# A decode attention kernel that streams its cache: a branch at the head of TensorE's program, and five sets of small loads

## The chip, the cores and the metric

The kernel runs on one core of a Trainium2 chip. The metric is the device time of one execution in microseconds (us); lower is better. A profile is one execution taken by the hardware profiler. It names the engines PE (TensorE; PEld is its weight load), DVE (VectorE), ACT (ScalarE), POOL (GpSimd) and SP (SyncE, which here only issues transfers and waits). Transfers run on the core's 16 DMA engines, whoever issues them.

## The reference, cut to what matters

One decode step for two sequences: attention with 32 query heads over 8 cached key and value heads of 32768 positions each, gated by a small network. Everything is float32, and each element of the caches is read once.

```python
xn = _layernorm(x)                                   # x: 2 x 1 x 512
q  = (xn @ wq) as 2 x 32 heads x 128
k, v = caches, each of 2 x 8 heads x 32768 x 128     # 4 query heads share one
p  = softmax(q k^T / sqrt(128));  o = p v
s  = o @ wo
h  = relu(xn @ w1 + b1) ** 2
return x + s * silu(h @ w2 + b2)
```

## The kernel before

All weights and both caches are packed on the host into matrices of 128 rows, and SP loads them in the order of their use through two slots in SBUF of 128 x 16384 floats (8.4 MB each). The stream has 66 loads: `wq`, then `wm` (the two matrices of the small network), and then, for each of the 16 pairs of sequence and cached head, two halves of the keys (`kt`) and two halves of the values (`vt`). Behind the last load SP issues seven pieces of `wo` (4 MB down to 128 KB), which lie in a buffer of their own.

A load may be issued when the matmuls that read its slot two loads earlier are done. `load` (L163 to L170) makes SP wait for the token of those matmuls and then issue; `release` (L177 to L188) is called where such a block of matmuls ends and issues the next load. SP's program is thus a row of waits and issues. Its counter `issued[0]` holds the number of loads so far, the one being issued included.

PE, ACT and DVE do not run through unrolled code. The class `Looped` records their operations (so that every recorded operation has line L63), and after all is recorded, three parts are emitted for each of them: what stands ahead of the loop (`ahead`), a hardware loop of 16 rounds whose body is one pair (`round`), and what follows (`rest`).

- Ahead of the loop: layer norm; the queries from the first load (`sc<-slot,xT`), transposed (`tp`); the small network from the second load (`wb<-slot,xT`, `wb<-slot,hT`, `wb<-o_sb,selq`).
- A round: the scores of both key halves into two PSUM banks (`sc<-slot,qz`); the row maximum, spread by a transpose (`ms<-ident,r`); the exponential on ACT; transposes of the probabilities (`tp<-ident,prob`); the sums (`ms<-selh,l`); the values times the probabilities (`o_ps<-slot,pT`); a transpose and a sum of the partial results (`ot<-ident,o_sb`).
- After the loop: `wo` times the heads (`wb<-wo_sb,oT` and `sc<-wo_sb,oT`), as its pieces arrive; then the gate, the residual and the store.

A matmul in float32 of this program stands in the trace as two matmuls, each with a weight load. The loop is opened with `head_slot={PE: 0}`, which makes its first instruction the first of a block of 256 instructions: an alignment mark and a branch stand ahead of it (the `ISA` and `UNCONDITIONAL_BRANCH` of L449).

Of the kernel before, what the change touches and what calls it, by code (L numbers as in the profile page):

```python
# [124 lines left out]
def build(nc, x22, x8, kt, vt, wq, wm, wo, out):  # L125
    pe, act, dve = (Looped(nc, e, n) for e, n in ((nc.tensor, "pe"), (nc.scalar, "act"), (nc.vector, "dve")))
    pool, sp = (Engine(nc, e, n) for e, n in ((nc.gpsimd, "pool"), (nc.sync, "sp")))
# [7 lines left out]
    def sb(name, *shape):  # L135
        return nc.alloc_sbuf_tensor(name, [P, *shape], F32)
# [18 lines left out]

    slot_sem = [nc.alloc_semaphore(f"slot{i}") for i in range(NSLOT)]
    piece_sem = [nc.alloc_semaphore(f"piece{i}") for i in range(len(PIECES) + 2)]
    small_sem, xe_sem, out_sem = (nc.alloc_semaphore(n) for n in ("small", "xe", "out"))
    count = [0] * NSLOT
    free = [None] * NSLOT  # L160
    issued = [0]

    def load(src, width):  # L163
        i = issued[0] % NSLOT
        issued[0] += 1
        if free[i] is not None:
            sp.wait(free[i])
        count[i] += 16
        nc.sync.dma_start(slots[i][:, 0:width], src).then_inc(slot_sem[i], 16)  # L169
        return i, (slot_sem[i], count[i])  # L170

    stream = [load(wq, SLOT)]
    nc.sync.sem_clear(out_sem)
    stream.append(load(wm, 2 * FJ * D))
    todo = [(x[s, u], SLOT) for s in range(NS) for x in (kt, vt) for u in range(2)]

    def release(token):  # L177
        free[stream.pop(0)[0]] = token
        if todo:
            stream.append(load(*todo.pop(0)))  # L180
            if not todo:
                h = 0
                for n, sem in zip(PIECES, piece_sem):
                    nc.sync.dma_start(wo_sb[:, h * D:(h + n) * D], wo[h * P:(h + n) * P].rearrange("(p h) e -> p (h e)", h=n)).then_inc(sem, 16)
                    h += n
                for u in range(2):
                    nc.sync.dma_start(wo_sb[:, h * D + u * NG * HN:h * D + (u + 1) * NG * HN],
                                      wo[h * P + u * HN:h * P + (u + 1) * HN].rearrange("r (t e) -> (r t) e", t=2)).then_inc(piece_sem[len(PIECES) + u], 16)  # L188
# [3 lines left out]
    t = pool.done(g.memset(ident[:, :], 0.0))  # L192
# [11 lines left out]
    for u in range(2):  # L204
# [5 lines left out]
    t = dve.done("tensor_reduce", selh[:, :], ident[:, :].rearrange("p (a h) -> p h a", h=REP), axis=AX.X, op=ALU.add)  # L210
# [10 lines left out]
    t = pe.done()  # L221
    dve.wait(t)
    t = dve.done("tensor_copy", xs[:, :], ms[:, 0:22])
    pe.wait(t, t_one)
    mm(ms[:, 32:40], mean[:, :], xs[:, 0:8], start=True, stop=True)
    t = pe.done()
    dve.wait(t)
    t = dve.done("tensor_reduce", st[:, 2:4], ms[:, 32:40].rearrange("p (d b) -> p b d", b=B), axis=AX.X, op=ALU.add)
    dve.wait(t)
    t = dve.done("tensor_tensor", xc[:, :].rearrange("p (d b) -> p d b", b=B), xs[:, 0:8].rearrange("p (d b) -> p d b", b=B),  # L230
                                 st[:, None, 2:4].to_broadcast([P, ND, B]), op=ALU.add)
    dve.wait(t)
    t = dve.done("tensor_mul", sq[:, :], xc[:, :], xc[:, :])
    pe.wait(t)
    mm(ms[:, 64:72], mean[:, :], sq[:, :], start=True, stop=True)
    t = pe.done()
    dve.wait(t)
    t = dve.done("tensor_reduce", st[:, 4:6], ms[:, 64:72].rearrange("p (d b) -> p b d", b=B), axis=AX.X, op=ALU.add)
    dve.wait(t)
    t = dve.done("tensor_scalar", st[:, 6:8], st[:, 4:6], -1.0, 1e-5, op0=ALU.mult, op1=ALU.add)  # L240
    act.wait(t)
    t = act.done("activation", st[:, 8:10], st[:, 6:8], AF.Sqrt)
    dve.wait(t)
    t = dve.done("reciprocal", st[:, 10:12], st[:, 8:10])
# [5 lines left out]
    i, t = stream[0]  # L250
# [6 lines left out]
    t = pe.done()  # L257
# [3 lines left out]
    for f in range(2):  # L261
# [3 lines left out]
        t = pe.done()  # L265
# [14 lines left out]
    def scores(u):  # L280
        i, t = stream[0]
        pe.wait(t, t_set, t_exp[u])
        for j in range(NJ):
            for c in range(NG):
                lo = (c * NJ + j) * W
                mm(sc[u][32 * c:32 * c + 32, :], qz[:, 28 - 4 * j:60 - 4 * j], slots[i][:, lo:lo + W],
                         start=(j == 0), stop=(j == NJ - 1))
        t = pe.done()
        release(t)
        dve.wait(t)  # L290
        return t, dve.done("tensor_reduce", rm[:, u:u + 1], sc[u][:, :], axis=AX.X, op=ALU.max)
# [44 lines left out]
    for s in range(NS):  # L336
# [4 lines left out]
        t_s, t = scores(1)  # L341
# [3 lines left out]
        t = dve.done("tensor_reduce", r1[:, :], rm[:, :], axis=AX.X, op=ALU.max)  # L345
        pe.wait(t, *([t_rs] if t_rs else []))
        tr(ms[:, :P], r1[:, :].to_broadcast([P, P]), ident[:, :])
        t = pe.done()
        dve.wait(t)
        t = dve.done("tensor_reduce", mh[:, :], ms[:, :P].rearrange("p (a h) -> p h a", h=REP), axis=AX.X, op=ALU.max)  # L350
        dve.wait(t)
        t = dve.done("tensor_mul", mm4[:, :], mh[:, :], seln[:, :])
        dve.wait(t)
        t = dve.done("tensor_reduce", nm[:, :], mm4[:, :], axis=AX.X, op=ALU.add)
# [5 lines left out]
        for u in range(2):  # L360
# [3 lines left out]
            t = pe.done()  # L364
# [4 lines left out]
        t = pe.done()  # L369
        dve.wait(t)  # L370
        t_rs = dve.done("reciprocal", rs[:, :], ms[:, :REP])
        for u in range(2):
            i, t = stream[0]
            pe.wait(t, t_pT[u], t_osb)
            for n in range(32):
                y = n % NG
                k, r = divmod(n, 8)
# [36 lines left out]
    for n, sem in zip(PIECES, piece_sem):  # L414
        pe.wait((sem, 16))
        for h in range(h, h + n):
            if h < WIDE:
                c = h % NG
                mm(wb[32 * c:32 * c + 32, :], heads(h, 0), wt[:, h, :], start=(h < NG), stop=(h >= WIDE - NG))
                if h == WIDE - 1:  # L420
                    t = pe.done()
# [15 lines left out]
    t = pe.done()  # L437
    dve.wait(t, t_gate)
    t = dve.done("tensor_mul", yb[:, :], gate[:, :], acc[:, :HN])
    dve.wait(t, (xe_sem, 32))  # L440
    t = dve.done("tensor_add", yb[:, :], yb[:, :], xb[:, :HN])
    sp.wait(t)
    nc.sync.dma_start(out, yb[:, :]).then_inc(out_sem, 16)
    used = sorted(x.num for x in [e.sem for e in (pe, act, dve, pool, sp)] + slot_sem + piece_sem + [small_sem, xe_sem])
    nc.sync.sem_clear(range(used[0], used[-1] + 1))
    nc.sync.wait_ge(out_sem, 16)
    for e in (pe, act, dve):
        e.ahead()
    with nc.Fori(0, NS, 1, engines=OrderedEngineSet([e.e.engine for e in (pe, act, dve)]), head_slot={pe.e.engine: 0}) as i:  # L449
# [46 lines left out]
```

## Time and profile before

| What | us |
|---|---|
| median of 3 runs | 1303.39 |
| lowest and highest | 1303.38, 1303.41 |
| span of the profiled execution | 1301.8 |
| PE matmul busy | 672.3 |
| PE weight loads busy | 208.2 |
| ACT busy | 78.9 |
| DVE busy | 49.5 |

The span runs from the first to the last instruction of the program in the profile. The runs are timed without a profiler and hold a little more at both ends, so the table has both. Over the span the core reads 561.01 MB, a mean of 431 GB/s. Shares of the DMA engines are means over all 16; a share of 0.25 can be four engines at work or sixteen at a quarter. A packet is put down to the stretch in which it starts or runs by its own times, so that in very short stretches a share can pass 1.

### The profile page before, as it was taken

The page shows a single profiled execution, that of the slowest core. Times are in us where ns is not written, and L with a number is a line of the kernel's source. Part 1 is how long each engine was busy: PE and PEld are TensorE (multiplying, and loading weights), DVE is VectorE, ACT ScalarE, POOL GpSimd, SP SyncE. Part 2 cuts the span into 40 slices and gives each one's busy share as a digit, 9 for nine tenths or more (in the row PEclk, how much of TensorE's full clock was granted, in tenths as well). Part 3 has the DMA queues.
Part 4 walks back from the last instruction along what each step waited for, and adds up shares of the span by engine and source line. Part 5 has one row for each costly group of instructions (what it writes and reads, how often), then busy time and mean ns, then how long its engine had stood idle before and what let it go on. Part 6 is the DMA issues. An engine that isn't in the chain of part 4 may idle for free.

```text
span 1301.8 us, 10286 instructions
## 1 busy us (share of the span) xinstructions
PE 672.3 (52%) x4671; PEld 208.2 (16%) x4671; DVE 49.5 (4%) x166; ACT 78.9 (6%) x138; POOL 5.4 (0%) x29
## 2 busy tenths in 40 slices
PE   3456455535546545545635544554554654554565
PEld 1111111201112111111212111111111211111122
DVE  0000000000000000000000000000000000000000
ACT  1010010100001010010101001010010101001010
POOL 0000000000000000000000000000000000000000
PEclk9776667677677778677767767767767767767778
DMA  9999999999999999999999999999999999999998
GB/s 406 433 446 423 445 423 447 419 441 429 429 441 427 443 425 445 423 447 419 439 431 427 443 427 443 425 445 421 447 421 439 431 427 443 427 443 425 445 421 362
DMA packets 10726, 561.13 MB, mean 431 GB/s; under 512 B 1339, under 2 KB 1633, under 8 KB 1889
## 3 DMA queue, kind: packets, MB, share of 16 engines
q1 hardware_dynamic: 10656, 561.03, 99.7%
q8 instruction: 5, 0.08, 0.0%
q10 hardware_dynamic: 65, 0.02, 0.0%
HBM read 561.01 MB, written 0.03 MB: 431 GB/s over the span
## 4 chain that ended last, share of the span: by engine, by line
DMA 75%; PE 24%; issue 1%; DVE 0%; ACT 0%; SPq 0%; DVEq 0%; ACTq 0%
DMA slot<-in_vt 36%; DMA slot<-in_kt 36%; PE sc L63 12%; PE o_ps L63 11%; DMA slot<-in_wm 3%; PE wb L63 1%; DVE hT L63 0%; PE ot L63 0%; DVE o_sb L63 0%; ACT o_sb L63 0%; DVE yb L63 0%; SPq L169 0%; DVE t L63 0%; DVE oT L63 0%; DVEq L101 0%
## 5 line engine op out<-in xcount | busy, mean ns | idle before, releaser
L63 PE MATMUL sc<-slot,qz 128*32 128x512 f32 x2048 | 295.3, 741 | 300.0 <-DMA slot<-in_kt 300.0
L63 PE MATMUL o_ps<-slot,pT 128*16 128x512 f32 x2048 | 294.3, 739 | 208.9 <-DMA slot<-in_vt 208.9
L63 PEld LDWEIGHTS sc<-slot,qz 128*32 128x32 f32 x2048 | 81.1, 133 | 503.4 <-issue 503.4
L63 PEld LDWEIGHTS o_ps<-slot,pT 128*16 128x16 f32 x2048 | 69.3, 113 | 420.6 <-issue 420.6
L63 ACT ACT_TABLE_LOAD x19 | 24.4, 1283 | 650.5 <-DVE nm L63 647.6
L63 PE MATMUL tp<-ident,prob 128*128 128x128 f32 x136 | 31.0, 397 | 53.3 <-ACT prob L63 53.2
L63 DVE TENSOR_REDUCE rm<-sc 128x1 f32<-128x512 f32 x32 | 22.1, 692 | 575.1 <-PE sc L63 575.1
L63 ACT COPY o_sb<-o_ps 128x512 f32<-128x512 f32 x16 | 9.4, 585 | 504.7 <-PE o_ps L63 504.7
L63 PEld LDWEIGHTS tp<-ident,prob 128*128 128x128 f32 x136 | 23.8, 204 | 57.9 <-issue 56.1
L63 DVE TENSOR_REDUCE t<-ot 128x4 f32<-128x64 f32 x16 | 3.6, 224 | 524.0 <-PE ot L63 524.0
L63 ACT ACTIVATE prob<-sc,nm 128x512 f32<-128x512 f32 x32 | 21.7, 682 | 0.2
L63 ACT COPY pT<-tp 128x512 f32<-128x512 f32 x32 | 18.7, 585 | 13.8 <-PE tp L63 13.8
L63 PE MATMUL sc<-slot,xT 128*32 128x512 f32 x64 | 8.4, 684 | 17.5 <-DMA slot<-in_wq 17.5
L63 PE MATMUL ot<-ident,o_sb 128*128 128x128 f32 x64 | 10.1, 280 | 13.7 <-ACT o_sb L63 13.7
L63 PEld LDWEIGHTS ms<-selh,l 128*128 128x128 f32 x64 | 15.6, 334 | 0.0
L63 PE MATMUL ms<-ident,r 128*128 128x128 f32 x16 | 4.7, 294 | 20.0 <-DVE r L63 20.0
L63 PE MATMUL ms<-selh,l 128*128 128x4 f32 x64 | 13.7, 319 | 0.0
L63 PEld LDWEIGHTS ot<-ident,o_sb 128*128 128x128 f32 x64 | 6.7, 141 | 27.9 <-issue 27.9
L63 PE MATMUL wb<-slot,xT 128*32 128x448 f32 x32 | 4.6, 738 | 6.6 <-DMA slot<-in_wm 6.6
L273 POOL COPY qz<-qT 128x4 f32<-128x4 f32 x16 | 3.0, 186 | 1167.3 <-PE sc L63 1137.3
L63 PEld LDWEIGHTS ms<-ident,r 128*128 128x128 f32 x16 | 2.1, 133 | 34.1 <-issue 34.1
L63 PE MATMUL wb<-wo_sb,oT 128*32 128x512 f32 x54 | 6.2, 596 | 0.7 <-DVE oT L63 0.7
(62 smaller groups left out, 55.6 us busy)
## 6 DMA issues: line engine op xcount, KB each, us to landing
slot<-in_wm SPq DMA_DIRECT2D x1, 7168.0 KB, 38.3
wo_sb<-in_wo SPq DMA_DIRECT2D x1, 4096.0 KB, 39.3
wo_sb<-in_wo SPq DMA_DIRECT2D x1, 2048.0 KB, 43.7
wo_sb<-in_wo SPq DMA_DIRECT2D x1, 1024.0 KB, 45.8
slot<-in_kt SPq DMA_DIRECT2D x32, 29.2
slot<-in_vt SPq DMA_DIRECT2D x32, 29.2
wo_sb<-in_wo SPq DMA_DIRECT2D x1, 512.0 KB, 46.6
wo_sb<-in_wo SPq DMA_DIRECT2D x1, 256.0 KB, 46.7
```

The source lines that it names most:

```text
L63: instruction = getattr(self.e, name)(*[x(i) if callable(x) else x for x in args], **kw)
L273: return pool.done(g.tensor_copy(qz[:, 28:32], qT[:, b, hkv, :]))
```

## The change

Three things are added.

- PE's program gets an alignment mark for a block of 256 instructions at its head, and PE, ACT and DVE a branch to a new part, `second_block`, in which all that was there before follows. The padding that the alignment needs is jumped over.
- Behind the loads with the numbers 3, 4, 6, 8 and 42 SP issues fifteen small loads, for k = 1 to 15: k rows of 16 + k floats (68 to 124 bytes a row) from `wo` into a buffer `mark` that nothing reads.
- SP's last wait, ahead of the store of the result, waits for these 75 loads too.

```diff
+    mark, mark_sem = sb("mark", 75, 32), nc.alloc_semaphore("mark")
...
         nc.sync.dma_start(slots[i][:, 0:width], src).then_inc(slot_sem[i], 16)
+        if issued[0] in (at := (3, 4, 6, 8, 42)):
+            for k in range(1, 16):
+                nc.sync.dma_start(mark[0:k, 15 * at.index(issued[0]) + k - 1, 0:16 + k], wo[0:k, 0:16 + k]).then_inc(mark_sem, 16)
         return i, (slot_sem[i], count[i])
...
-    sp.wait(t)
+    sp.wait(t, (mark_sem, 5 * 15 * 16))
     nc.sync.dma_start(out, yb[:, :]).then_inc(out_sem, 16)
...
     nc.sync.wait_ge(out_sem, 16)
+    nc.tensor.addr_align(256, offset=0, max_nops=0)
+    nc.br("second_block", engines=OrderedEngineSet([e.e.engine for e in (pe, act, dve)]))
+    nc.switch_bb("second_block")
     for e in (pe, act, dve):
         e.ahead()
```

The instructions in their order show where the additions stand. First PE, from the start of its program to the scores of the loop's first key half; before:

```order
L63 MATMUL ms<-ident,small 128x22
L63 MATMUL ms<-xs,mean 128x8
L63 MATMUL ms<-sq,mean 128x8
L63 MATMUL sc<-slot,xT 32x512 x32
L63 MATMUL tp<-ident,prob 128x128 x8
L63 MATMUL wb<-slot,xT 32x448 x16
L63 MATMUL wb<-slot,hT 32x512 x14
L63 MATMUL wb<-o_sb,selq 32x64 x8
L449 ISA
L449 UNCONDITIONAL_BRANCH
```

The same place now:

```order
L451 ISA
L452 UNCONDITIONAL_BRANCH
L63 MATMUL ms<-ident,small 128x22
L63 MATMUL ms<-xs,mean 128x8
L63 MATMUL ms<-sq,mean 128x8
L63 MATMUL sc<-slot,xT 32x512 x32
L63 MATMUL tp<-ident,prob 128x128 x8
L63 MATMUL wb<-slot,xT 32x448 x16
L63 MATMUL wb<-slot,hT 32x512 x14
L63 MATMUL wb<-o_sb,selq 32x64 x8
L456 ISA
L456 UNCONDITIONAL_BRANCH
```

Nothing changes its place against its neighbours; all of it starts at the head of a block. Then SP's row around the fourth load (`slot` is a slot of the stream, `in_wo` the weights in HBM):

```order
L173 DMA mark<-in_wo 13x29
L173 DMA mark<-in_wo 14x30
L173 DMA mark<-in_wo 15x31
L170 DMA slot<-in_kt 128x16384
L173 DMA mark<-in_wo 1x17
L173 DMA mark<-in_wo 2x18
L173 DMA mark<-in_wo 3x19
```

The end of the set behind the third load is followed by the fourth load, which waits for its slot as before, and by the next set; the fifth load then stands behind that.

More of the change, by code (lines that the diff above doesn't have):

```diff
@@ L441, in build @@
     t = dve.done("tensor_add", yb[:, :], yb[:, :], xb[:, :HN])
-    sp.wait(t)
+    sp.wait(t, (mark_sem, 5 * 15 * 16))
     nc.sync.dma_start(out, yb[:, :]).then_inc(out_sem, 16)
-    used = sorted(x.num for x in [e.sem for e in (pe, act, dve, pool, sp)] + slot_sem + piece_sem + [small_sem, xe_sem])
+    used = sorted(x.num for x in [e.sem for e in (pe, act, dve, pool, sp)] + slot_sem + piece_sem + [small_sem, xe_sem, mark_sem])
     nc.sync.sem_clear(range(used[0], used[-1] + 1))
     nc.sync.wait_ge(out_sem, 16)
+    nc.tensor.addr_align(256, offset=0, max_nops=0)
+    nc.br("second_block", engines=OrderedEngineSet([e.e.engine for e in (pe, act, dve)]))
+    nc.switch_bb("second_block")
     for e in (pe, act, dve):
```

## The prediction

> **What bounds the kernel now.** I read the page first, then the chain of waits, then the DMA view and the view of stretches where the chain left a question. The page says that the 16 DMA engines are full from the first microseconds to the last slice, nearly all of it from queue q1, which SP issues; q8 is the queue that brings instructions.
>
> ```profile
> PE 672.3 (52%) x4671; PEld 208.2 (16%) x4671; DVE 49.5 (4%) x166; ACT 78.9 (6%) x138; POOL 5.4 (0%) x29
> ...
> DMA  9999999999999999999999999999999999999998
> q1 hardware_dynamic: 10656, 561.03, 99.7%
> q8 instruction: 5, 0.08, 0.0%
> ```
>
> The chain of waits (start, length, what) shows the same thing from the other side. It changes between a load in flight and the block of matmuls that frees the slot for the load after next.
>
> ```profile
> 79.97 8.86 PE sc L63 x64
> 88.83 0.02 issue
> 88.84 29.71 DMA slot<-in_vt
> 118.56 0.22 issue
> 118.77 9.92 PE o_ps L63 x64
> 128.69 0.02 issue
> 128.71 28.54 DMA slot<-in_kt
> 157.25 0.12 issue
> ...
> 1279.65 0.22 issue
> ...
> 1299.78 0.23 DVE yb L63
> ```
>
> Landings at 118.56 and 157.25 are two loads apart: 38.69 us, or 19.35 us a load. Yet a load is issued 28.5 to 29.7 us before it lands, so it waits about 10 us behind the load ahead of it, and the engines never run dry. The 24% of the chain that is put down to PE is therefore cover, not cost. The time is set by the DMA engine that has most to do, plus the 22 us behind the last landing at 1279.65, where PE works through the last scores and the last weights.
>
> Is one engine later than the others? The stretches at the end answer it. Their columns are the stretch, its length, busy time of PE, PEld, DVE, ACT and POOL, the granted clock, the DMA share and GB/s.
>
> ```profile
> 1296.80:1297.00 0.20, 0.20 (x8) 0.20 (x8) 0.00 (x0) 0.00 (x0) 0.00 (x0) 1.00 1.02 353
> 1297.20:1297.40 0.20, 0.20 (x7) 0.08 (x3) 0.00 (x0) 0.00 (x0) 0.00 (x0) 1.00 0.33 123
> 1297.60:1297.80 0.20, 0.20 (x7) 0.05 (x4) 0.00 (x0) 0.00 (x0) 0.00 (x0) 1.00 0.26 102
> 1298.40:1298.60 0.20, 0.20 (x27) 0.20 (x18) 0.00 (x0) 0.17 (x1) 0.00 (x0) 1.00 0.26 92
> 1298.60:1298.80 0.20, 0.20 (x26) 0.20 (x20) 0.00 (x0) 0.00 (x0) 0.00 (x0) 1.00 0.11 36
> ```
>
> Until 1297.0 all sixteen work. Then the share falls to 0.26, which is 4 of 16, and stays there until about 1298.6. Four engines end some 1.5 us behind the other twelve. What they did more is in the DMA view of four short stretches, 43 to 46, 55 to 58, 89 to 92 and 125 to 129 us, in this order:
>
> ```profile
> q8 instruction: 1, 0.02, 2.1%
> q8 instruction: 1, 0.02, 2.0%
> q8 instruction: 1, 0.02, 2.0%
> q8 instruction: 1, 0.02, 1.6%
> ```
>
> Each stretch holds one instruction packet of 16 KB, and 2.0% of 16 engines over 3 us is 1.0 us on one engine. Four fetches in the stream and four late engines: I take it that each fetch made one engine late, by the 1.0 us and some 0.5 us of disturbance. The fifth fetch comes at the very end.
>
> **The change part by part.** *The branch.* PE's program ahead of the loop is 153 matmuls (1+2+2+64+8+32+28+16), each with its weight load, so 306 instructions, over one block of 256; behind the loop stand 150 (54+80+16), and the page's count leaves (4671-153-150)/16 = 273 matmuls, 546 instructions, for a round. Its part of the timeline (start, busy, name, count, idle before it):
>
> ```profile
> 2.95 0.26 PE L63 MATMUL ms<-ident,small 22*128 22x22 f32 x1 [2.95 <-DMA small<-in_x]
> 22.83 8.38 PE L63 MATMUL sc<-slot,xT 128*32 128x512 f32 x64 [17.48 <-DMA slot<-in_wq]
> 39.65 4.64 PE L63 MATMUL wb<-slot,xT 128*32 128x448 f32 x32 [6.59 <-DMA slot<-in_wm]
> 46.39 3.63 PE L63 MATMUL wb<-slot,hT 128*32 128x512 f32 x28 [2.10 <-DVE hT L63]
> 50.70 0.43 PE L63 MATMUL wb<-o_sb,selq 128*32 128x64 f32 x16 [0.69 <-ACT o_sb L63]
> ```
>
> The jump itself and any fetch behind it fall into the first 2.95 us, and behind those stand 17.48 us in which PE waits for the first load: cost 0. Without that cover it would be one fetch, 1.0 us, and its way through the queue. The branches of ACT and DVE move the small loads by at most a tenth of a microsecond, under the same cover.
>
> Now the fetches. The times fit a fetch that starts one block ahead whenever PE enters a block: 44 us while the program ahead of the loop runs, 56 at the loop, 90 and 126 at the two block borders within the loop's first round. With the program pushed to the start of a block, entering it brings one fetch at about 1 us, before or beside the first load; its 306 instructions cross one border at the matmuls of 46.39, and the loop, at the start of a block as before, gives the last three again. So four fetches remain in the stream, one of them a few us later, and one more stands at the start. In the loop nothing moves. Bounds: 0 if the fetch at the start is out of the way when the first load comes or its engine isn't the last, 1.5 us if it lands on one of the four. I take 0. If the fetch ahead of the loop holds PE up, it may last until the third load lands, near 60.5 (one load ahead of the landing at 79.85), some 9 us behind 51.1, with nothing late.
>
> [...]
>
> *The marks on SP.* SP's issue of a small load, and its waits (line, releaser, total, times, longest):
>
> ```profile
> L184 SPq DMA_DIRECT2D wo_sb<-in_wo x5: 432/432/433, 1250.0 to 1251.9; - x5
> SPq L169 <- PE sc L63: 637.2, 33, 29.6
> SPq L169 <- PE o_ps L63: 570.6, 30, 19.6
> ```
>
> Fifteen at 0.43 us are 6.5 us of SP per set. SP waits 1207.8/63 = 19 us before each load, and the marks follow a load, ahead of the next wait; a set is issued before the next slot comes free. Cost 0; were the cover gone, 6.5 us a set, less the 10 us by which loads are early.
>
> *The marks on the DMA engines.* Here nothing hides them: an engine that carries a mark starts its share of the next load later, and lateness is never made up. A mark of k rows gives k data packets and its semaphore packets. How many marks meet on one engine no row tells; from 0 to 75 (15 in each of five sets). The price of one mark on one engine lies between these rows: eight 512-byte packets of the small loads in the stretch 12 to 13 us, eight 4-byte semaphore packets in 9.6 to 10.1, and the landings of the last weights.
>
> ```profile
> q10 hardware_dynamic: 8, 0.00, 1.4%
> q10 hardware_dynamic: 8, 0.00, 0.9%
> wo_sb<-in_wo SPq DMA_DIRECT2D x1, 4096.0 KB, 39.3
> wo_sb<-in_wo SPq DMA_DIRECT2D x2, 128.0 KB, 46.5
> L187 SPq DMA_DIRECT2D wo_sb<-in_wo x2: 418/424/431, 1252.4 to 1252.9; - x2
> ```
>
> 1.4% of 16 us over eight is 28 ns, 0.9% of 8 us over eight is 9 ns. So data of 68 to 124 bytes and a semaphore cost at least 2 x 9 = 18 ns and at most 28 + 9 = 37 ns while back to back. For the ceiling: the 4096 KB piece lands at 1250.0 + 39.3 = 1289.3, the last one at 1252.9 + 46.5 = 1299.4. Between them lie six transfers of 4096 KB in all, 4.194 MB, which at the stream's rate (8.389 MB in 19.35 us, 433.5 GB/s) take 9.67 us of those 10.1. The rest is 0.07 us a transfer. I take 20 ns, since a mark is nearer to 4 bytes than to 512, and 60 marks: not all 75 need meet a late engine, but the one of the four that carries most decides, so the value lies high. 60 x 0.020 = 1.2 us.
>
> [...]
>
> *The end.* SP waits for the marks' semaphore too before the last store, long reached: one more instruction in the row, 0.02 to 0.1 us by the chain's issue pieces (0.02 to 0.22); I take 0.05. Behind the last landing nothing else moves, and a late engine moves it and PE's last blocks alike.
>
> The sum: 0 + 0 + 1.2 + 0.05 = 1.25 us on the profiled 1301.8, thus 1303.05. The runs' median, 1303.39, holds 1.6 us more than the span, and I carry that over: 1303.39 + 1.25 = **1304.6 us**.
>
> **The rivals.** *Dear marks* (slower). A mark holds its engine for the ceiling, since it must wait for its own write before the next goes. 60 to 75 marks at 0.07 us are 4.2 to 5.3 us: 1307.6 to 1308.7; if only the middle of 0.045 us, 1306.1. It decides over 0.2% from 0.043 us a mark. Against it: of the 0.07 us much belongs to eight packets, not one.
>
> *A full queue* (slower). Before, at most nine transfers stood open at once (two loads and seven pieces of weights, whose issues show no stall at 432 ns). Now it is seventeen. If SP could push no more than nine, seven marks would wait until the load ahead of them ends; then come 7 x 0.43 = 3.0 us of issue and a cold start of the next load, which took 22.0 - 19.35 = 2.65 us for the first load:
>
> ```profile
> slot<-in_wq SPq DMA_DIRECT2D x1, 22.0
> ```
>
> 5.65 us five times is 28 us: 1332. From sixteen places on it costs nothing, because the load in flight ends before the next slot is released. For it speaks only that the trace never had more than nine.
>
> *The marks miss* (no slower). The engines that carry the marks are not those that the fetches hit, and twelve engines have 1.5 us of slack: 0.05 us remain, 1303.4. If the moved fetches also spare an engine that is late for other reasons, part of the 1.5 us returns: down to 1301.9. That is not yet 0.2%. For it: twelve of sixteen engines have slack. Against: four are hit, and the worst counts.
>
> *The branch changes nothing*, where the program's start stands already at a block's border or the fetch goes elsewhere: then the marks' term stands alone, within the forecast.
>
> **How the numbers follow.** Forecast (+0.3 to +2.6 us): 0.57. Marks miss: 0.14. Dear marks: 0.17. Full queue: 0.09. Faster by over 0.2%, for which I know no mechanism, since the whole lag of the late engines is 1.5 us: 0.03. A bound of 0.2%, 2.6 us, is about what a measurement can tell; it lies at 1300.8 and 1306.0. Faster 0.03, same 0.57 + 0.14 = 0.71, slower 0.17 + 0.09 = 0.26. The range leaves out the full queue, the gain beyond half of the lag, and the far end of dear marks: 1302.6 (half the lag returned) to 1307.6 (60 marks at the ceiling).
>
> **What would show it.** After: q1 at 99.7% of the engines still; landings 19.35 us apart, and up to 0.3 us more behind a load with marks; SP's marks at about 0.43 us each without a hole, and its waits shorter by 6.5 us five times; one q8 packet near 1 us, four until 130 us; at the end a staircase in the DMA share in place of the step to 0.26, its foot 1 to 2 us later than 1298.6. It is wrong if the DMA share drops behind a set of marks (full queue), if the last landing moves by over 3 us (dear marks), or if it moves forward.

## The result, and the profile after

The changed kernel takes 1312.49 us (median of three, 1312.19 to 1312.58) against 1303.39: a ratio of 1.0069, 95% interval 1.0051 to 1.0087. That is 9.1 us more, outside the predicted range of 1302.6 to 1307.6. The profiled execution has a span of 1310.9 us, 9.1 more than before, so its trace holds the whole loss.

The page of the changed kernel: DMA by slices, all packets, and the queues.

```profile
DMA  9999999999999999999999999999999999999997
...
DMA packets 11928, 561.22 MB, mean 428 GB/s; under 512 B 2539, under 2 KB 2833, under 8 KB 3089
...
q1 hardware_dynamic: 11856, 561.09, 99.4%
q8 instruction: 6, 0.10, 0.0%
...
q14 instruction: 1, 0.01, 0.0%
```

The packets under 512 bytes are 1200 more than the 1339 of before: 600 rows of the small loads and 600 completions. They bring 0.06 MB, and but for the last slice the engines are as full as before. So the time is not lost in a hole that a slice could show; it looks as if some engine has more to do.

Where it has more to do is read from the chain of waits: the piece in front of each block of matmuls starts where a load has landed, here every second load (4, 6, 8, 10, 12, and then 42 and 44). Before, from load 10 on (4, 6 and 8 follow from the chain in the prediction):

```profile
195.95 0.22 issue
...
234.65 0.12 issue
...
815.19 0.22 issue
...
853.88 0.12 issue
```

After, from load 4 on:

```profile
80.53 0.12 issue
...
121.05 0.22 issue
...
162.08 0.12 issue
...
202.78 0.22 issue
...
241.50 0.12 issue
...
822.36 0.22 issue
...
863.07 0.12 issue
```

| load | 4 | 6 | 8 | 10 | 12 | 42 | 44 |
|---|---|---|---|---|---|---|---|
| landing before | 79.85 | 118.56 | 157.25 | 195.95 | 234.65 | 815.19 | 853.88 |
| landing after | 80.53 | 121.05 | 162.08 | 202.78 | 241.50 | 822.36 | 863.07 |
| later by | 0.68 | 2.49 | 4.83 | 6.83 | 6.85 | 7.17 | 9.19 |

Without a set, two loads are 38.7 us apart in both kernels (202.78 to 241.50). With a set between them they are 40.5 to 41.0. Each of the last four sets costs the slowest engine 1.8 to 2.3 us; of the first, only 0.68 us show, because other engines were some 1.5 us late already. What is lost stays lost until the end: 9.2 us of lateness behind the fifth set are the 9.1 us of the result.

The trace also has the step that each of the sixteen engines adds to a load's semaphore when its share has landed. Before, twelve engines end load 66 by 1278.09 us and four at 1279.39 to 1279.65, as the prediction had read from the shares. After, they end one after another from 1282.49 to 1288.83. Even the first is 4.8 us later than before, since by the program a slot is given on only when a load has landed on all engines and has been read. A run below, in which one engine alone carries small loads, has the same: 1282.61 to 1284.45 for fifteen engines, 1289.20 for the last.

SP is not the cause. Its timeline (start, us, line, operation, count):

```profile
33.40 0.33 SPq L170 DMA_DIRECT2D slot<-in_kt  x1
33.78 5.36 SPq L173 DMA_DIRECT2D mark<-in_wo  x15
53.91 0.36 SPq L170 DMA_DIRECT2D slot<-in_kt  x1
54.31 5.24 SPq L173 DMA_DIRECT2D mark<-in_wo  x15
68.83 20.81 SPq L170 DMA_DIRECT2D slot<-in_vt  x2
```

Fifteen small loads are issued in 5.2 to 5.4 us, and SP is done long before the next slot comes free.

At the end the step of before has become a long foot (the same columns as in the prediction):

```profile
1305.60:1306.00 0.40, 0.07 (x4) 0.07 (x7) 0.00 (x0) 0.00 (x0) 0.00 (x0) 1.00 0.19 72
1306.40:1306.80 0.40, 0.40 (x6) 0.15 (x3) 0.00 (x0) 0.00 (x0) 0.00 (x0) 1.00 0.12 44
1307.20:1307.60 0.40, 0.40 (x32) 0.40 (x32) 0.00 (x0) 0.40 (x1) 0.00 (x0) 1.00 0.07 26
1307.60:1308.00 0.40, 0.40 (x40) 0.40 (x34) 0.00 (x0) 0.07 (x1) 0.00 (x0) 1.00 0.06 20
```

A share of 0.19 is three engines, 0.06 is one: the engines end one after another, one of sixteen still loads the last pieces when all others have ended, and TensorE waits for such a piece (0.07 of 0.40 us busy in the first row).

### The profile page after: what moved, and what is told of

It is laid out like the page before. It is cut to its first block, busy times and chain, and to the rows that moved or that the text cites. A ratio compares the mean times of both kernels' runs of the same rounds, so it can differ in the third digit from the quotient of the medians.

```text
span 1310.9 us, 10363 instructions
## 1 busy us (share of the span) xinstructions
PE 680.5 (52%) x4671; PEld 209.6 (16%) x4671; DVE 49.5 (4%) x166; ACT 78.9 (6%) x138; POOL 5.4 (0%) x29
## 4 chain that ended last, share of the span: by engine, by line
DMA 76%; PE 23%; issue 0%; DVE 0%; SPq 0%
DMA slot<-in_kt 36%; DMA slot<-in_vt 34%; PE sc L63 11%; PE o_ps L63 11%; DMA wo_sb<-in_wo 3%; DMA slot<-in_wm 3%; PE wb L63 1%; DVE hT L63 0%; SPq L188 0%; SPq L170 0%; DVE o_sb L63 0%; DVE yb L63 0%; SPq L177 0%
## 5 line engine op out<-in xcount | busy, mean ns | idle before, releaser
L63 DVE TENSOR_REDUCE rm<-sc 128x1 f32<-128x512 f32 x32 | 22.1, 692 | 575.6 <-PE sc L63 575.6
## 6 DMA issues: line engine op xcount, KB each, us to landing
wo_sb<-in_wo SPq DMA_DIRECT2D x1, 4096.0 KB, 38.7
```

The costliest lines, as they stand in the source:

```text
L63: instruction = getattr(self.e, name)(*[x(i) if callable(x) else x for x in args], **kw)
```

## The experiments

All but the first start from the changed kernel. The kernel before, timed beside them, took 1303.41 us (1303.53 beside the last four). The branch alone, the small loads alone and the 75 spread loads have medians of 10, 4 and 10 runs, which differ by up to 0.9 us among themselves; each of the others is a single run.

**The two halves of the change.** The first is the kernel before with the branch and no small loads, the second the changed kernel without the branch.

```diff
+    nc.tensor.addr_align(256, offset=0, max_nops=0)
+    nc.br("second_block", engines=OrderedEngineSet([e.e.engine for e in (pe, act, dve)]))
+    nc.switch_bb("second_block")
```

> The branch and the alignment without the small loads. If the small loads made all of the 9.1 us (my theory), this is within 1 us of before: 1302.8 to 1304.2, with one instruction packet near 2 us and four until 130 us. If the moved fetches or a late start of TensorE make a part, it is slower by that part: 1306 and more.

```diff
-    nc.tensor.addr_align(256, offset=0, max_nops=0)
-    nc.br("second_block", engines=OrderedEngineSet([e.e.engine for e in (pe, act, dve)]))
-    nc.switch_bb("second_block")
```

> The small loads without the branch. My theory: 1312 to 1313.5, the whole loss; the landings of the big loads fall back by some 2 us behind each of the five sets. If the loss needs both parts, clearly less: 1304 to 1309.

Measured: 1303.5 us for the branch alone, ratio 1.0001 (0.9991 to 1.0010), and 1312.41 for the small loads alone, ratio 1.0068 (1.0051 to 1.0085). The small loads are the whole loss. The instruction queue with the branch alone, in the stretches 0 to 3, 52 to 55, 60 to 63, 89 to 92 and 125 to 129 us:

```profile
q8 instruction: 1, 0.02, 2.3%
q8 instruction: 1, 0.02, 2.0%
q8 instruction: 1, 0.02, 2.1%
q8 instruction: 1, 0.02, 2.1%
q8 instruction: 1, 0.02, 1.7%
```

One fetch more, at the start, and four in the stream as before. The one at the start did make an engine late: the last engine ends load 2 at 40.40 us in place of 39.60. At the end of the stream four engines land later than that one (1279.13 to 1279.36 against 1278.87 in load 66), and no time is lost.

**Packets or transfers.** Each set becomes one transfer of 16 rows with 15 short pieces in each, so that every engine gets fifteen short packets, but one completion.

```diff
-            for k in range(1, 16):
-                nc.sync.dma_start(mark[0:k, 15 * at.index(issued[0]) + k - 1, 0:16 + k], wo[0:k, 0:16 + k]).then_inc(mark_sem, 16)
+            n = 15 * at.index(issued[0])
+            nc.sync.dma_start(mark[0:16, n:n + 15, 0:24], wo[0:16, 0:480].rearrange("p (c e) -> p c e", e=32)[:, :, 0:24]).then_inc(mark_sem, 16)
...
```

> Each set is one transfer of 16 rows with 15 pieces of 96 bytes in each: as many short packets on every DMA engine as the fullest engine had before, but one completion in place of fifteen. If a set is dear because each transfer is completed by itself (theory A, 0.14 us a transfer), five sets cost 5 x (0.14 + 15 x 0.01), 1.5 us: 1304 to 1305.5. If short packets are dear in themselves (theory B), the loss stays on all engines: 1312 to 1315.

Measured: 1305.27. Five sets cost 1.9 us, 0.37 us each, on all engines alike (the first and the last engine end load 66 2.4 and 2.2 us later than before). Fifteen short packets in one transfer are cheap, 0.025 us each if the one completion costs nothing; fifteen transfers are dear.

**The length of a row.** Rows of 512 bytes, into a part of the `wo` buffer, whose own loads SP holds back until these have landed.

```diff
-... mark[0:k, 15 * at.index(issued[0]) + k - 1, 0:16 + k], wo[0:k, 0:16 + k]
+... wo_sb[0:k, 128 * (15 * at.index(issued[0]) + k - 1):128 * (15 * at.index(issued[0]) + k)], wo[0:k, 0:128]
...
+                sp.wait((mark_sem, 5 * 15 * 16))
```

> The same 75 transfers with the same rows, each row 512 bytes in place of 68 to 124, written to a part of the wo buffer that is loaded over later. Theory A (a price per transfer, whatever its bytes up to some kilobytes): unchanged, 1312 to 1313.5. Theory B (writes under 512 bytes are dear): 75 packets of 28 + 9 ns on the fullest engine, 2.8 us: 1304.5 to 1307.

Measured: 1314.83, more than either expectation. Longer rows don't help, so it isn't the shortness of a row; the 2.3 us on top are 0.03 us for each of 75 transfers, twice the 0.015 us that 416 bytes more take at 433.5 GB/s over sixteen engines. The rest is not explained.

**What a transfer could be waiting for.** Three kernels: a semaphore of its own for each of the fifteen loads of a set; a source in SBUF (`mean`, a constant tile) in place of HBM; one row in each load, so that the set touches as few engines as it can.

```diff
-... .then_inc(mark_sem, 16)
+... .then_inc(mark_sem[k - 1], 16)
...
```

> As in the change, but the fifteen loads of a set count on fifteen semaphores in place of one. Theory A1, the completion of each transfer holds its engine: unchanged, 1312 to 1313. Theory A2, sixteen engines get in each other's way at one semaphore: most of the loss goes, 1304 to 1307.

```diff
+            sp.wait(t_one)
-... wo[0:k, 0:16 + k]
+... mean[0:k, 0:16 + k]
```

> The small loads read a constant tile in SBUF in place of wo in HBM, otherwise the same. Theory A1 (completion): unchanged, 1312 to 1313. Theory A3, each transfer waits for its own read from HBM: clearly less, 1304 to 1308.

```diff
-... mark[0:k, 15 * at.index(issued[0]) + k - 1, 0:16 + k], wo[0:k, 0:16 + k]
+... mark[0:1, 15 * at.index(issued[0]) + k - 1, 0:16 + k], wo[0:1, 0:16 + k]
```

> Each of the 75 small loads has one row in place of 1 to 15, 75 data packets in all in place of 600. If one DMA engine pays for each transfer by itself and the fullest engine sets the end: unchanged, 1312 to 1313, with the loads' landings falling back behind each set as before. If the price came from many engines together (600 packets, 600 completions): 1304 to 1306.

Measured: 1312.39, 1312.64 and 1312.57. None of the three matters: not the shared semaphore, not the read from HBM, not the number of engines. The last run is the plainest view of the mechanism. Its DMA view from 120.2 to 120.45 us, within which the set behind load 6 is read:

```profile
DMA packets 33, 0.13 MB, mean 530 GB/s; under 512 B 31, under 2 KB 31, under 8 KB 31
```

and its chain around that set:

```profile
79.98 0.12 issue
...
120.70 0.25 issue
...
161.45 0.12 issue
```

All fifteen rows and the packets that complete them start within a quarter of a microsecond, one load every 0.014 us, near the 0.018 us that I had costed at the least. So the engine had all fifteen loads at hand. Yet the next loads land 2.0 us late (40.72 and 40.75 in place of 38.7). The starts of these packets tell nothing of when the engine is free of them. The trace also records when a completion reaches its semaphore. Those of this set follow the landing of load 6 at 120.70 us from 120.89 to 123.50, one load after the other, 0.18 to 0.19 us apart.

**How many at once.** Five, thirty, and the same 75 spread over 25 places.

```diff
-            for k in range(1, 16):
+            for k in range(1, 6):
...
```

> Only the loads of 1 to 5 rows in each set: 25 transfers, all of which touch the fullest engine. With a fixed price of 0.144 us a transfer, and 1.5 us by which the engines hit by fetches are later than that engine: 25 x 0.144 - 1.5, 2.1 us, 1305 to 1306. If the first few transfers behind a big load are free and only the later ones dear (the short packets start 14 ns apart at first, and later some 0.1 us apart): 1303.2 to 1304.2.

```diff
-            for k in range(1, 16):
-                nc.sync.dma_start(mark[0:k, 15 * ...
+            for p, k in [(p, k) for p in (0, 64) for k in range(1, 16)]:
+                nc.sync.dma_start(mark[p:p + k, 15 * ...
...
```

> Thirty small loads a set in place of fifteen (the second fifteen go to 64 partitions further on). Completions 0.187 us apart with 0.7 us covered once a set: 5 x (5.6 - 0.7) - 1.5, 23 us: 1325 to 1328. A price of 0.14 us for each transfer without a covered part: 150 x 0.14 - 1.5, 1322 to 1324. If SP's queue held fewer than some 30 transfers, holes in its issue and more than 1330.

```diff
-        if issued[0] in (at := (3, 4, 6, 8, 42)):
-            for k in range(1, 16):
+        if 3 <= issued[0] < 28:
+            for n in range(3 * issued[0] - 9, 3 * issued[0] - 6):
+                k = n % 15 + 1
...
```

> The same 75 small loads, three behind each of the loads 3 to 27 in place of fifteen behind five. Theory A with a hidden part: small transfers complete 0.187 us apart on one engine, and of each set some 0.7 us are covered by what the engine still has to write; three make 0.56 us, so nothing is left: 1303.0 to 1304.0. If each transfer has a price of its own wherever it stands (0.14 us, less 1.5 us of slack): 1311 to 1313.

Measured: 1303.08 with five, 1327.06 with thirty, 1303.91 with 75 spread (ratio 1.0004, 0.9994 to 1.0013). The time with five is a little under both expectations: five a set don't show in it. A constant price for each would have made 1305 or more. The chain with thirty, at loads 8 and 10, with one set between them:

```profile
171.01 0.12 issue
...
214.50 0.25 issue
```

43.49 us against 40.70 for fifteen at the same place: 2.79 us for fifteen transfers more, 0.186 us each, the spacing of the completions. Fifteen would then be 2.79 us and cost 2.00 (40.70 less 38.70), so about 0.8 us of a set are covered. Three spread loads take 0.56 us and stay below that, and of the 9.1 us at most 0.4 are left though every transfer of the change is there. That is the strongest of the runs. It doesn't show that such loads are free: with the 1.5 us by which other engines are late anyway, up to 1.9 us can hide in it, 0.03 us for each of 75, against 0.13 us in sets of fifteen. Why those 0.8 us are covered, the runs don't show.

**Why the ceiling of the prediction was none.** It came from the last pieces of `wo`. Two kernels put larger transfers in the place of the small ones: fifteen of 128 rows of 64 bytes, and ten of 128 rows of 1 KB, the form of those last pieces.

```diff
-... mark[0:k, 15 * at.index(issued[0]) + k - 1, 0:16 + k], wo[0:k, 0:16 + k]
+... mark[:, 15 * at.index(issued[0]) + k - 1, 0:16], wo[0:128, 0:16]
```

> Fifteen transfers a set as in the change, but each of 128 rows of 64 bytes, so eight packets on each of the 16 engines. Theory A, one completion each 0.187 us whatever the packets: 5 x (2.8 - 0.7), 10.5 us, now on the engines too that the fetches make late: 1313 to 1315. If each packet is waited for: 5 x 15 x 8 x 0.187, over 100 us. If only the packets' own time counted (8 x 0.014 a transfer): 5 x (1.7 - 0.7), 1308 to 1309.

```diff
-            for k in range(1, 16):
-... mark[0:k, 15 * at.index(issued[0]) + k - 1, 0:16 + k], wo[0:k, 0:16 + k]
+            for k in range(1, 11):
+... wo_sb[:, 256 * (10 * at.index(issued[0]) + k - 1):256 * (10 * at.index(issued[0]) + k)], wo[0:128, 0:256]
...
+                sp.wait((mark_sem, 5 * 10 * 16))
...
```

> Ten transfers a set of 128 rows of 1 KB, the form of the last pieces of wo, from which I took the ceiling of 0.07 us: 8 KB on each engine. Their data alone is 5 x 10 x 0.303, 15.1 us. If the completion runs beside the next transfer's data (my reason why the ceiling was none): 15.1 + 5 x 10 x 0.05, 1320 to 1322. If it is added to the data, 0.187 each: 1327 to 1329.

Measured: 1319.2 and 1321.88. The second fits: 18.4 us over before, of which 15.1 are data; the other 3.3 us are 0.07 us for each of 50 transfers, the very number of the prediction. So a transfer with 8 KB on each engine costs 0.07 us beyond its data, and one of about a hundred bytes 0.186 us. I read it as a completion that runs beside the data of the next transfer in the one case and has nothing to run beside in the other; no run shows that, they have the two sizes only. The first missed all its expectations and is not clean, because SP stalls in it:

```profile
33.48 0.33 SPq L170 DMA_DIRECT2D slot<-in_kt  x1
33.86 27.07 SPq L173 DMA_DIRECT2D mark<-in_wo  x15
60.98 0.43 SPq L170 DMA_DIRECT2D slot<-in_kt  x1
61.45 21.61 SPq L173 DMA_DIRECT2D mark<-in_wo  x15
```

Fifteen issues take 27 us in place of 5.4, and the next big load goes out only at 60.98. In the second SP stalls as well, 25.04 us for the first ten. The next big load of each, from the chain of the first and from that of the second (start, us):

```profile
60.98 22.11 DMA slot<-in_kt
57.92 25.67 DMA slot<-in_kt
```

The load of the first kernel takes no longer than the first load of the program, into idle engines (22.0 in the prediction), and it lands within 0.65 us on all sixteen engines (82.44 to 83.09), so that even the lag of the late ones is gone: the engines had run dry. The load of the second still waits behind the pieces, and its late engines are still late (81.52 to 83.60). So the second is the cleaner of the two. How much of the 15.7 us of the first are the dry engines and how much eight packets a transfer, the run can't tell.

## Why the prediction was wrong

Its frame held. The DMA engine with most to do sets the end; the branch costs no time (1303.5 us alone, against 1303.41); one fetch more stands at the start and four stay in the stream (near 53, 61, 90 and 126 to 129 us; the first two come 9 and 5 us later than before, where I had told of one); SP hides the issue of the small loads (5.2 to 5.4 us a set); the wait at the end is too small to be seen. The direction was right as well, and so was the place: the small loads make an engine late, and lateness is not given back. The sign that the prediction gave for dear marks, a landing later by over 3 us, came with 9.2 us.

The step that failed is the price of a mark, that is, of a small load on its engine: "at least 18 ns and at most 37 ns while back to back", the ceiling of 0.07 us a transfer, and the 20 ns taken, which made 1.2 us in the sum. The runs give 0.186 us for each small transfer that follows another on its engine, with some 0.8 us of a set covered. Fifteen a set: 5 x (2.8 - 0.8) = 10 us, less the 1.5 us by which other engines were late already, is 8.5 us; measured are 9.1. The 60 marks that I took to meet the late engines are shown by no run, and were the wrong count too: the engine that all loads share carries 75 and became the last by itself, far past those that the fetches delay (behind the sets at loads 6, 8 and 42 the last completion comes 2.79 us after the landing, fifteen times 0.186).

Two readings led there. The lower bounds were packet times, and the run with one row shows that those say little of when the engine is free: 0.014 us from start to start, 0.186 from completion to completion. And the ceiling was taken from transfers of 8 KB an engine, where only 0.07 us of that time show. I had called it a bound from both sides; it was a bound only for transfers of that size. The rival of dear marks was nearest: it let each mark hold its engine, and the completions do follow one another 0.186 us apart. What the engine waits for (the rival says its own write) was not shown, and priced by the same ceiling it ended at 1308.7, still 3.8 us short.

The full queue, which I priced by the number of open transfers, did not appear with seventeen of them, nor did it cost with thirty: SP needed 15.50 us for one set there in place of 10.75, and the time still followed from the completions. It does exist where each transfer has eight packets on each engine: there fifteen issues took 27 us in place of 5.4, and the engines ran dry (22.1 us for the next big load, as for the first), as that rival said.

The runs put the price on the completion: one for fifteen packets is cheap (0.37 us a set), fifteen are dear (1.8 to 2.3 us for each of the last four sets), whatever the source (1312.64 us), the semaphore (1312.39) and the number of engines (1312.57, against 1312.49). Whether the 0.186 us are the confirmation of the data's write or the semaphore's own write was not separated, and every run writes to SBUF.

## What to carry to other kernels

Here small transfers in a stream that fills the DMA engines were priced by the transfer, hardly by the byte or the packet (0.03 us for 416 bytes more, 0.025 us for a packet in one transfer): 0.19 us each where they follow one another on an engine, and next to nothing in the time where three or five stand behind a big load (1303.91 and 1303.08 us, against 1303.53 and 1303.41). So make one transfer with many short pieces of them, or spread them between large ones. And take a price per transfer read from the profile for transfers of that size alone (here 0.07 us at 8 KB an engine, 0.186 at about a hundred bytes); before calling it a ceiling, ask what its time may have been hidden behind.

## What had not been expected of the hardware

- Starts and completions of small transfers run apart: fifteen loads start 0.014 us apart and complete 0.18 to 0.19 us apart.
- SP's issue stalled where many packets stood open: with eight packets on each engine the eighth transfer of a set took 12.22 us to issue, the seven ahead of it 0.43 to 0.48 each. Fifteen transfers with eight packets on each engine behind two big loads took 27 us to issue, ten with 8 KB on each engine 25 us; fifteen with one packet on the fullest engine took 5.4.
- The page after has one packet of 8 KB on q14, which the page of before has not. I take it for a fetch of SP's program, which is 75 transfers longer. The traces bear that out: the packet comes at 965 us with 25 small loads, at 690 with the 50 pieces, at 294 with 75, and with 150 there are two, at 102 and 1046.
